# Four attention layers on one core: the second normalising product moves from VectorE to GpSimd

## The chip, the cores and the metric

The kernel runs on one core of a Trainium2 chip. The metric is the device time of one launch in microseconds. The core has a matrix engine (TensorE, PE in the profile, with its weight loads shown as PEld), VectorE (DVE), ScalarE (ACT), GpSimd (POOL) and SyncE (SP). Each engine works through a queue of its own in order, and the engines wait for one another on semaphores. SP, ACT and POOL also issue DMAs; the kernel calls their DMA queues SP, AQ and GQ. A GpSimd instruction and a DMA issued from GpSimd stand in the same physical queue.

## The reference

The input is 2048 tokens of width 1024, bf16, with 32 heads of width 32. Four residual blocks follow one another, A, B, A, B, and the two A blocks share weights, as do the two B blocks.

```
x = x + A(layernorm(x));  x = x + B(layernorm(x))      # twice
A: q, k, v = x @ wqkv;  phi(t) = [softmax(t @ w_phi), softmax(-t @ w_phi)]
   o = (phi(q) @ (phi(k)^T v)) / (phi(q) . sum(phi(k)) + 1e-6);  o @ wo
B: q, k, v = x @ wqkv
   p = softmax(q k^T / sqrt(32));  o = p @ v;  o @ wo
```

Block A is a linear attention and is cheap. Block B is a full softmax attention over 2048 x 2048 scores in each of 32 heads.

## The kernel before

The program is written by a planner. Every piece of work is an `op(engine, planned duration, function, dependencies, buffers, priority)`. The class `Sched` plays the whole program through once on the host, engine by engine, with planned durations, latencies (`LAT`) and buffers that come free (`QUOTA` limits how many of a class live at once), and emits the instructions in the order in which they start in that play. That order is what each hardware queue then holds. The planner treats POOL (instructions) and GQ (DMAs issued by GpSimd) as two engines; the hardware has one queue for both. `TIE` seeds a random draw that multiplies each planned DVE and PE duration by a factor between 0.99 and 1.01; another seed, or another list of DVE and PE operations, gives another order throughout the program.

Activations are held transposed (features on partitions) in chunks of 512 tokens. A block B, in `attention`, is 32 turns: one turn is a query chunk `qc` (4 of them) with a group `g` of four heads (8 of them). A turn has two halves `pp`, and each half 32 units; a unit is the scores of one head, 128 keys by 512 queries.

- Scores: TensorE writes groups of two or three units to PSUM (L1257).
- Exponentials: most groups go to ScalarE (L1273, 1536 or 1024 columns wide). Some units go to VectorE, which computes the exponential with a polynomial (`exp_dve`): `take` reads PSUM (L1184), then five instructions on SBUF follow for a pair of units (L1193, L1196, L1198, L1201, L1203). How many is fixed by the table `COUNT`.
- Weighted sums: TensorE multiplies the exponentials by v and by ones (L1305) into one PSUM bank. After each half VectorE copies that bank to a buffer `T` in SBUF (L1321): 64 partitions hold sums over v and the other 64 the denominators, the other way round in the other half.
- Normalising: four small DMAs gather the denominators of both halves, VectorE takes reciprocals (L1361), one DMA writes them to DRAM and one reads them back spread over the partitions (`bk`). Two products follow (L1370): the first, `k = 1`, over all 128 partitions with the `T` of the second half, and then `k = 0` over the lower 64 partitions with the `T` of the first half. Both write the same bf16 tile `oT`, so the second waits for the first. The lower half of what the first wrote is overwritten.

The last turn of each attention is normalised in another way and has no L1370, so there are 31 turns with two products in each of the two attentions.

The output projection reads `oT` much later in most turns. While the attention runs, TensorE also makes keys, queries and values of later head groups (L530, copied out of PSUM by VectorE at L1057 and L1065). In the first attention there are also layer norms (L691, L695) and the keys of the next block A for three chunks (L820 to L841), where GpSimd casts a column of reciprocals (L841). GpSimd's other work in these stretches is issuing weight loads (L705, L709).

Of the kernel before, what the change touches and what calls it, by code (L numbers as in the profile page):

```python
# [52 lines left out]
OVER = {"DVE": 0.085, "ACT": 0.012}  # L53
NEXT = {"DVE": 0.05, "ACT": 0.13}
RING = 0.5
TIE = 17
LOOK = 8


# [10 lines left out]
class Sched:  # L70
# [11 lines left out]
    def op(self, eng, dur, fn, deps=(), bufs=(), prio=0.0, lat=None, mode=None):  # L82
        o = Op(eng, dur, LAT[eng] if lat is None else lat, fn, tuple(bufs), prio, mode, len(self.ops))
        for d in deps:
            if d is not None:
                d.out.append(o)
                o.ndep += 1
        for b in o.bufs:
            b.left += 1
        if eng == "DVE" and any(b.kind == "ps" and b.banks in ([(7,)], [(6,)]) for b in o.bufs):  # L90
            o.ahead = EVAC
        self.ops.append(o)
        return o
# [76 lines left out]
    def run(self):  # L170
        draw = random.Random(TIE)
        for o in self.ops:
            if TIE and o.eng in ("DVE", "PE"):
                o.dur *= 1 + draw.uniform(-0.01, 0.01)
# [193 lines left out]
def dve_us(n):  # L368
    return n / 960 + 0.15
# [6 lines left out]
def kernel(  # L376
# [11 lines left out]
    nc = tc.nc  # L388
# [95 lines left out]
    op = sch.op  # L484

    def sb(cls, *dims, dt=BF16):
        n = 1
        for d in dims:
            n *= d
        b = Buf("sb", -(-n * (4 if dt == F32 else 2) // 64) * 64, cls)  # L490
        b.with_ = ()

        def v():
            ap = arena[:, b.at // 2:b.at // 2 + n * (2 if dt == F32 else 1)]
            if dt == F32:
                ap = ap.bitcast(F32)
            if len(dims) == 2:
                ap = ap.rearrange("p (a b) -> p a b", a=dims[0])
            elif len(dims) == 3:
                ap = ap.rearrange("p (a b c) -> p a b c", a=dims[0], b=dims[1])  # L500
            return ap

        return b, v
# [707 lines left out]
    def attention(base, kT, vT, q_of, gate, extra):  # L1211
# [69 lines left out]
        if True:  # L1281
            for qc, g in turns:
                T = []
# [43 lines left out]
                r_b, r_v = d_b, d_v  # L1327
                if end:

                    o_b, o_v = sb("oT", C512)  # L1330
# [3 lines left out]
                    s = [op("DVE", dve_us(512), lambda o_v=o_v, r_v=r_v, T=T: nc.vector.tensor_tensor(  # L1334
                        out=o_v()[lo_, :], in0=T[0][1]()[lo_, :], in1=r_v()[hi_, :], op=ALU.mult),
                        rc, [o_b, d_b, T[0][0]], prio)]
# [10 lines left out]
                    s = cut[0] + cut[1][-1:]  # L1347
# [19 lines left out]
                o_b, o_v = sb("oT", C512)  # L1367
                s = []
                for k, a in ((1, slice(0, P)), (0, lo_)):
                    s.append(op("DVE", dve_us(512), lambda a=a, k=k, o_v=o_v, r_v=r_v, T=T: nc.vector.tensor_tensor(  # L1370
                        out=o_v()[a, :], in0=T[k][1]()[a, :], in1=r_v()[a, :], op=ALU.mult),
                        [bk, *s], [o_b, r_b, T[k][0]], prio))
                oTs[qc][g] = (o_b, o_v, s)
# [23 lines left out]
    for layer in range(2):  # L1397
# [48 lines left out]
        for c in range(NC):  # L1446
            pr = second + 20 * c
            o_b, o_v = sb("oc", G, C512)
# [38 lines left out]
        if wide == NC:  # L1487
            for i in range(pos[(2, HALF)], len(turns)):
                qc, g = turns[i]
                pl = at + 10 * i - LATE  # L1490
                wl = slab("w2", pl - 3, B_w[:, :, g * P:(g + 1) * P], P, [q_of[turns[i - 2]][2][0]])
                q_of[(qc, g)] = b_q(g, qc, pl, wl, FIL)
        oTs, last_s = attention(at, kT, vT, q_of, gate, lambda i: PAIRS[COUNT[layer][i]])
        if last:
            bo_s = [slab("slab", at + BO + fc, B_o[:, :, fc * C512:(fc + 1) * C512], C512, [q_of[(1, G - 1)][2][0]])
# [27 lines left out]
        if not last:  # L1523
            r_b, r_v = sb("w2r", 2, D)
# [68 lines left out]
```

## Time and profile before

| | |
|---|---|
| time before, median of 3 runs | 2245.67 us (2244.37 to 2248.56) |
| time of the profiled execution | 2247.36 us |
| its span, first to last instruction | 2245.1 us |
| busy: PE, DVE, ACT, POOL | 2176.1, 1855.9, 1985.7, 197.0 us |
| mean granted TensorE clock | 0.998 |
| first attention's exponentials on ScalarE | from 327 us to the stretch 1200 to 1250 us |
| second attention's exponentials on ScalarE | from the stretch 1400 to 1450 us to 2234 us |

The busy time of an engine is the time in which at least one of its instructions is under way, as a sum over stages with different limits. Durations of neighbouring VectorE instructions overlap a little in the records, so the step from start to start is shorter than the duration. The profiled execution took 2.3 us more than its span, and 1.7 us more than the median.

### The profile page before, as it was taken

The page shows a single profiled execution, that of the slowest core. Times are in us where ns is not written, and L with a number is a line of the kernel's source. Part 1 is how long each engine was busy: PE and PEld are TensorE (multiplying, and loading weights), DVE is VectorE, ACT ScalarE, POOL GpSimd, SP SyncE. Part 2 cuts the span into 40 slices and gives each one's busy share as a digit, 9 for nine tenths or more (in the row PEclk, how much of TensorE's full clock was granted, in tenths as well). Part 3 has the DMA queues.
Part 4 walks back from the last instruction along what each step waited for, and adds up shares of the span by engine and source line. Part 5 has one row for each costly group of instructions (what it writes and reads, how often), then busy time and mean ns, then how long its engine had stood idle before and what let it go on. Part 6 is the DMA issues. An engine that isn't in the chain of part 4 may idle for free.

```text
span 2245.1 us, 82636 instructions
## 1 busy us (share of the span) xinstructions
PE 2176.1 (97%) x36788; PEld 872.2 (39%) x36788; DVE 1855.9 (83%) x2761; ACT 1985.7 (88%) x1939; POOL 197.0 (9%) x299
## 2 busy tenths in 40 slices
PE   7999999999999999999999999999999999999999
PEld 4554454444333333333333444433333333333333
DVE  7986873698899889677887788799999999988968
ACT  4436669999999999999998555999999999999998
POOL 1110000000001010121124200000000000100000
PEclk9999999999999999999999999999999999999999
DMA  9220101111122221222235100111111100211111
GB/s 207 49 81 3 33 24 42 41 34 34 51 57 88 74 73 54 64 96 73 78 110 152 59 5 10 36 37 38 36 29 29 35 24 19 73 31 35 47 36 38
DMA packets 121789, 119.67 MB, mean 53 GB/s; under 512 B 57752, under 2 KB 99800, under 8 KB 121432
## 3 DMA queue, kind: packets, MB, share of 16 engines
q1 hardware_dynamic: 102392, 56.64, 10.0%
q0 software_dynamic: 17424, 56.18, 8.7%
q8 instruction: 287, 4.70, 0.9%
q10 hardware_dynamic: 1616, 1.57, 0.2%
q14 instruction: 70, 0.57, 0.1%
HBM read 79.23 MB, written 14.14 MB: 42 GB/s over the span
## 4 chain that ended last, share of the span: by engine, by line
PE 28%; ACT 23%; DVE 9%; issue 5%; DMA 1%; SPq 0%; ACTq 0%; DVEq 0%
ACT arena L1273 22%; PE psum L530 14%; PE psum L1305 6%; PE psum L1257 6%; DVE arena L1203 2%; DVE arena L1184 1%; DVE arena L1196 1%; DVE arena L1201 1%; DVE arena L1193 1%; ACT arena L823 1%; DMA arena<-arena 1%; DVE arena L1370 1%; DVE arena L1198 1%; DVE arena L1057 1%; PE psum L994 0%
## 5 line engine op out<-in xcount | busy, mean ns | idle before, releaser
L1273 ACT ACTIVATE arena<-psum 128x1536 bf16<-128x1536 f32 (+1 forms) x1366 | 1668.5, 1446 | 12.0 <-PE psum L1257 7.1
L530 PE MATMUL psum<-arena 128*32 128x512 bf16 (+1 forms) x18432 | 1058.3, 358 | 12.5 <-DVE arena L836 2.7
L530 PEld LDWEIGHTS <-arena 128*32 128x32 bf16 x18944 | 459.8, 96 | 447.2 <-issue 175.7
L1305 PE MATMUL psum<-arena 128*32 128x512 bf16 x4096 | 628.1, 383 | 4.0 <-issue 2.0
L1305 PE MATMUL psum<-arena,ones_bf 128*32 128x512 bf16 x4096 | 628.1, 383 | 0.0
L1257 PE MATMUL psum<-arena 32*128 32x512 bf16 x4096 | 536.2, 383 | 27.2 <-ACT arena L1273 22.4
L1257 PEld LDWEIGHTS <-arena 32*128 32x128 bf16 x4096 | 158.4, 91 | 555.8 <-issue 549.0
L1184 DVE TENSOR_SCALAR arena<-psum 128x512 int32<-128x512 f32 x418 | 284.5, 686 | 101.7 <-PE psum L1257 90.3
L1203 DVE SCALAR_TENSOR_TENSOR arena<-arena 128x1024 int16<-128x1024 int32 x209 | 254.7, 1218 | 5.7 <-DVE arena L1201 0.4
L1305 PEld LDWEIGHTS <-arena 128*32 128x32 bf16 x4096 | 163.2, 95 | 227.8 <-issue 177.0
L1305 PEld LDWEIGHTS <-ones_bf 128*32 128x32 bf16 x4096 | 161.3, 95 | 22.3 <-issue 7.9
L705 POOL DMA_DIRECT2D arena<-in_B_wqkv_dram x46 | 42.2, 919 | 1248.6 <-PE psum L530 302.5
L1193 DVE TENSOR_SCALAR arena<-arena 128x1024 f16<-128x1024 int16 x209 | 143.8, 690 | 4.4 <-DMA arena<-arena 0.3
L1196 DVE TENSOR_TENSOR arena<-arena 128x1024 f16<-128x1024 f16 x209 | 142.6, 684 | 4.6
L1201 DVE TENSOR_TENSOR arena<-arena 128x1024 f16<-128x1024 f16 x209 | 142.6, 684 | 3.1
L1057 DVE CAST arena<-psum 128x512 bf16<-128x512 f32 x128 | 87.7, 685 | 57.6 <-PE psum L530 57.3
L823 ACT ACTIVATE arena<-psum 128x512 bf16<-128x512 f32 x80 | 43.0, 596 | 82.6 <-PE psum L530 66.7
L827 DVE TENSOR_REDUCE arena<-arena 128x32 f32<-128x1024 bf16 x64 | 77.0, 1214 | 33.3 <-ACT arena L823 33.2
L530 PE MATMUL psum<-xT,onesD 128*32 128x512 bf16 x1144 | 103.1, 381 | 1.3 <-DVE arena L836 0.7
L1321 DVE COPY arena<-psum 128x512 f32<-128x512 f32 x126 | 86.3, 685 | 15.4 <-PE psum L1305 15.0
L1198 DVE TENSOR_SCALAR arena<-arena 128x1024 f16<-128x1024 f16 x209 | 87.9, 422 | 1.7
L836 DVE TENSOR_TENSOR arena<-psum,arena 128x1024 bf16<-128x1024 f32 x64 | 77.4, 1219 | 13.3 <-PE psum L530 9.7
(124 smaller groups left out, 1383.6 us busy)
## 6 DMA issues: line engine op xcount, KB each, us to landing
arena<-rd SPq DMA_DIRECT2D x62, 256.0 KB
arena<-in_B_wqkv_dram POOLq DMA_DIRECT2D x58, 256.0 KB, 4.1
arena<-in_B_wo_dram POOLq DMA_DIRECT2D x40, 256.0 KB, 4.4
arena<-arena SPq DMA_DIRECT2D x256, 32.0 KB
arena<-wd_k POOLq DMA_DIRECT2D x32, 256.0 KB, 5.0
arena<-in_A_wqkv_dram POOLq DMA_DIRECT2D x32, 256.0 KB, 4.6
arena<-arena SPq DMA_DIRECT2D x96, 64.0 KB
arena<-arena SPq DMA_DIRECT2D x248, 2.0 KB
```

The source lines that it names most:

```text
L530: nc.tensor.matmul(out_[ks, :], lhsT=lhsT[:, ks], rhs=rhs, start=start, stop=stop, tile_position=(0, 32 * k), skip_group_check=True)
L1057: return op("DVE", dve_us(512), lambda: nc.vector.tensor_copy(out=dst(), in_=src()), [dep], bufs, prio)
L1184: o = op("DVE", dve_us(512), lambda: nc.vector.tensor_scalar(out=x_v()[:, k, :].bitcast(I32), in0=s_v()[:, x * C512:(x + 1) * C512], scala ...
L1193: last = op("DVE", 1024 / 1920 + 0.15, lambda: nc.vector.tensor_scalar(out=z(), in0=x_v().bitcast(I16).rearrange("p a (n two) -> p a n two ...
L1196: last = op("DVE", 1024 / 1920 + 0.15, lambda: nc.vector.tensor_tensor(out=u(), in0=z(), in1=z(), op=ALU.mult), [last], [z_b, u_b], prio + ...
L1198: last = op("DVE", 1024 / 3840 + 0.15, lambda: nc.vector.tensor_scalar(out=u(), in0=u(), scalar1=POW2_C[0], scalar2=POW2_C[1], op0=ALU.mul ...
L1201: last = op("DVE", 1024 / 1920 + 0.15, lambda: nc.vector.tensor_tensor(out=u(), in0=z(), in1=u(), op=ALU.mult), [last], [z_b, u_b], prio + ...
L1203: return op("DVE", dve_us(1024), lambda: nc.vector.scalar_tensor_tensor(out=y_v().bitcast(I16), in0=x_v().bitcast(I32), scalar=128.0 / BIT ...
L1257: nc.tensor.matmul(out=s_v()[:, x * C512:(x + 1) * C512], lhsT=kT[g][1]()[r, pp, d * P:(d + 1) * P], rhs=q_of[(qc, g)][1]()[r, (pp + j // ...
L1273: ex = op("ACT", act_us(w * C512), lambda s_v=s_v, e_v=e_v, w=w: nc.scalar.activation(out=e_v(), in_=s_v()[:, 0:w * C512], func=ACT.Exp, s ...
L1305: nc.tensor.matmul(out=a_v()[col:col + 32, :], lhsT=v_v()[:, kc % 4, o:o + DH] if what == 0 else ones_bf[:], rhs=ev()[:, x * C512:(x + 1) ...
L1321: cp = op("DVE", dve_us(512), lambda t_v=t_v, a_v=a_v: nc.vector.tensor_copy(out=t_v(), in_=a_v()), [last], [a_b, t_b], prio - 4)
```

## The change

The second product (`k = 0`, 64 partitions by 512 columns, fp32 times fp32 to bf16, all in SBUF) is given to POOL with a planned duration of 1.3 us, in place of DVE with its planned 0.683 us. The seed `TIE` goes from 17 to 23.

```diff
-TIE = 17
+TIE = 23
...
                 for k, a in ((1, slice(0, P)), (0, lo_)):
-                    s.append(op("DVE", dve_us(512), lambda a=a, k=k, o_v=o_v, r_v=r_v, T=T: nc.vector.tensor_tensor(
+                    s.append(op("DVE" if k else "POOL", dve_us(512) if k else 1.3, lambda a=a, k=k, o_v=o_v, r_v=r_v, T=T: (
+                        nc.vector if k else nc.gpsimd).tensor_tensor(
                         out=o_v()[a, :], in0=T[k][1]()[a, :], in1=r_v()[a, :], op=ALU.mult),
                         [bk, *s], [o_b, r_b, T[k][0]], prio))
```

62 instructions move. Each now waits on a semaphore from VectorE for the first product, and the readers of `oT` wait for GpSimd.

## The prediction

> **What bounds the kernel now.** I read the page first, then the busy times by stretch, then ScalarE's waits, then the chain.
>
> ```profile
> span 2245.1 us, 82636 instructions
> PE 2176.1 (97%) x36788; PEld 872.2 (39%) x36788; DVE 1855.9 (83%) x2761; ACT 1985.7 (88%) x1939; POOL 197.0 (9%) x299
> ```
> ```profile
> core 0: us, PE busy (x) PEld busy (x) DVE busy (x) ACT busy (x) POOL busy (x), PEclk, DMA share, GB/s
> 1450.00:1550.00 100.00, 98.76 (x1505) 35.27 (x1502) 97.07 (x154) 99.57 (x85) 2.67 (x3) 1.00 0.14 33
> 1800.00:1900.00 100.00, 98.40 (x1543) 36.79 (x1543) 92.21 (x145) 100.00 (x86) 0.00 (x0) 1.00 0.09 23
> 900.00:950.00 50.00, 45.33 (x735) 16.00 (x731) 30.99 (x43) 47.03 (x42) 7.93 (x13) 0.97 0.25 71
> 1150.00:1200.00 50.00, 48.73 (x791) 17.73 (x788) 44.42 (x68) 47.11 (x43) 16.29 (x23) 0.97 0.30 85
> ```
> The page gives the base of all shares, 2245.1 us, and shows TensorE, ScalarE and VectorE all high, which an average over stages can't rank. The stretches can (columns: stretch, its length, then busy us and instructions of PE, PEld, DVE, ACT, POOL, then the granted clock). In the second attention ScalarE is busy for 99.57 and 100.00 of 100 us, TensorE for 98.76 and 98.40, VectorE for 97.07 and 92.21. In two stretches of the first attention ScalarE reaches only 47.03 and 47.11 of 50 us, and there the granted clock is 0.97.
>
> ```profile
> L1273 ACT ACTIVATE arena<-psum 128x1536 bf16<-128x1536 f32 (+1 forms) x1366 | 1668.5, 1446 | 12.0 <-PE psum L1257 7.1
> PE psum L1257 <- ACT arena L1273: 22.4, 77, 0.9
> ```
> ScalarE's exponentials stood idle for only 12.0 us in 1366 instructions, and TensorE's scores waited 77 times for ScalarE to free their bank. So ScalarE sets the pace of both attentions. Their exponentials are split between ScalarE and VectorE by a table which the change leaves alone. Work taken from VectorE shortens the run only where VectorE was, for a moment, what the others waited for. The chain tells how often that is:
>
> ```profile
> by line: ACT arena L1273 22.1%; PE psum L530 14.0%; PE psum L1305 6.4%; PE psum L1257 5.8%; issue 5.4%; DVE arena L1203 1.5%; DVE arena L1184 1.1%; DVE arena L1196 1.1%; DVE arena L1201 0.9%; DVE arena L1193 0.9%; ACT arena L823 0.8%; DMA a
> ```
> VectorE's polynomial lines lie on it with 1.5, 1.1, 1.1, 0.9 and 0.9 per cent each: small, but not nothing.
>
> **What leaves VectorE.** These groups show the moved product (64x512, x62) and what stands around it in VectorE's queue. The last figures are busy us, mean ns, idle us before.
>
> ```profile
> L1184 DVE TENSOR_SCALAR arena<-psum 128x512 int32<-128x512 f32 x418 | 284.5, 686 | 101.7 <-PE psum L1257 90.3 <-ACT arena L1273 4.9 <-ACT arena L1056 2.6
> L1203 DVE SCALAR_TENSOR_TENSOR arena<-arena 128x1024 int16<-128x1024 int32 x209 | 254.7, 1218 | 5.7 <-DVE arena L1201 0.4
> L1193 DVE TENSOR_SCALAR arena<-arena 128x1024 f16<-128x1024 int16 x209 | 143.8, 690 | 4.4 <-DMA arena<-arena 0.3
> L1201 DVE TENSOR_TENSOR arena<-arena 128x1024 f16<-128x1024 f16 x209 | 142.6, 684 | 3.1
> L1196 DVE TENSOR_TENSOR arena<-arena 128x1024 f16<-128x1024 f16 x209 | 142.6, 684 | 4.6
> L1198 DVE TENSOR_SCALAR arena<-arena 128x1024 f16<-128x1024 f16 x209 | 87.9, 422 | 1.7
> L1057 DVE CAST arena<-psum 128x512 bf16<-128x512 f32 x128 | 87.7, 685 | 57.6 <-PE psum L530 57.3
> L1321 DVE COPY arena<-psum 128x512 f32<-128x512 f32 x126 | 86.3, 685 | 15.4 <-PE psum L1305 15.0 <-ACT arena L1273 0.2
> L1370 DVE TENSOR_TENSOR arena<-arena 128x512 bf16<-128x512 f32 x62 | 42.1, 679 | 0.9 <-DMA arena<-rd 0.6 <-issue 0.2
> L1370 DVE TENSOR_TENSOR arena<-arena 64x512 bf16<-64x512 f32 x62 | 41.9, 675 | 0.1
> L1065 DVE TENSOR_SCALAR arena<-psum 128x512 bf16<-128x512 f32 x48 | 32.9, 685 | 19.4 <-PE psum L530 16.0 <-DMA arena<-rd 3.2
> ```
> ```profile
> 1621.44 0.68 DVE L1370 TENSOR_TENSOR arena<-arena 128x512 bf16<-128x512 f32 x1
> 1622.04 0.69 DVE L1193 TENSOR_SCALAR arena<-arena 128x1024 f16<-128x1024 int16 x1
> 1622.64 0.68 DVE L1370 TENSOR_TENSOR arena<-arena 64x512 bf16<-64x512 f32 x1
> 1623.25 0.68 DVE L1196 TENSOR_TENSOR arena<-arena 128x1024 f16<-128x1024 f16 x1
> ```
> The moved product lasts 675 ns, but from 1622.64 to 1623.25 it takes 0.61 us of the queue, and neighbours of its kind 0.60. So 62 x 0.60 = 37.2 us of VectorE's time go. The idle time before it is 0.1 us in all, so no wait goes with it. What it is worth is its share of the chain:
>
> ```profile
> 720.91 0.60 DVE arena L1370
> ...
> 2176.16 0.60 DVE arena L1370
> ```
> These are the first and the last of 15 pieces of the chain (start, us) that are second products; they sum to 8.2 us, 22% of 37.2. If nothing else changed, the gain would be at most 8.2 us, and less where ScalarE or TensorE is right behind.
>
> **What GpSimd needs for it.** The trace of before has no product of two SBUF tensors on GpSimd. The nearest rows:
>
> ```profile
> masks.py:199 POOL TENSOR_SCALAR_AFFINE_SELECT ident<-ident 128x128 bf16<-128x128 bf16 x1 | 0.3, 287 | 0.1
> L1577 POOL MEMSET const-bfloat16-1.0<- 128x1 bf16 x1 | 0.1, 101 | 0.0
> ```
> A row of 128 columns with one input takes 287 ns, and an instruction of one column 101 ns. That is (287 - 101) / 127 = 1.46 ns a column; 512 columns make 101 + 511 x 1.46 = 0.85 us for one input, and twice the column price, for two inputs, 1.60 us. I take 1.2 us, about the middle. The Trainium skill, GPSIMD Engine Reference, section Performance versus the Vector engine, gives about 2.6 cycles an element for two inputs, by which I estimate 512 x 2.6 / 1.2 GHz = 1.1 us plus dispatch; no run here shows it yet.
>
> GpSimd has time: it is busy 197.0 us of the run. The readers of `oT` are not in a hurry even at the end, where the margin is least:
>
> ```profile
> 2230.33 0.69 DVE L1370 TENSOR_TENSOR arena<-arena 128x512 bf16<-128x512 f32 x1
> 2232.19 0.67 DVE L1370 TENSOR_TENSOR arena<-arena 64x512 bf16<-64x512 f32 x1
> 2236.95 0.77 DVE L1344 TENSOR_TENSOR arena<-psum,arena 64x256 bf16<-64x256 f32 x2 [2.39 <-ACT arena L1342]
> ```
> At the end of the run the first product ends at 2231.02 and the second starts only at 2232.19, because another copy lies between. GpSimd could start right behind the first and end near 2231.1 + 1.2 = 2232.3 (2232.7 by the long price), ahead of today's 2232.86. Nor does the last turn's own product (L1344, at 2236.95) come any later, as it waits for ScalarE. I cost the tail at nothing; that cover holds as long as GpSimd's product ends before about 2236, and a product later than that moves the end by its lateness.
>
> **What it does to VectorE's other work.** This is the term that decides. The trace has both directions of a conflict between the two engines.
>
> ```profile
> L841 POOL CAST arena<-arena x64: 321/330/1129, 34.8 to 1261.0; 128x32 bf16<-128x32 f32 x64
> 100.09 1.16 DVE L695 TENSOR_TENSOR arena<-arena 128x1024 bf16<-128x1024 f32 x1
> 100.31 1.13 POOL L841 CAST arena<-arena 128x32 bf16<-128x32 f32 x1 [4.93 <-DVE arena L830]
> ```
> ```profile
> 1747.32 1.40 POOL L705 DMA_DIRECT2D arena<-in_B_wqkv_dram  x1 [50.78 <-DVE arena L1184]
> 1748.14 1.07 DVE L1193 TENSOR_SCALAR arena<-arena 128x1024 f16<-128x1024 int16 x1
> ```
> GpSimd's small cast (L841; min, median, max ns) takes 330 ns as a rule. The one at 100.31 took 1.13 us and ended at 101.44, 0.19 us after VectorE's L695 (two SBUF inputs) had ended at 101.25. GpSimd waited for the whole instruction. In the other direction VectorE's L1193, which takes 690 ns on average, took 1.07 us while GpSimd issued a DMA: 0.38 us were lost.
>
> So the two can't read together where VectorE has two SBUF inputs, or streams SBUF to SBUF at the pace of L1193 and L1198. In the groups above these are L1203, L1193, L1196, L1201, L1198 (5 x 209) and L1370 (124), 1169 instructions. Those that read PSUM are L1184, L1057, L1321 and L1065 (418 + 128 + 126 + 48 = 720). So 62% use what GpSimd needs. The product starts while VectorE goes on with its queue. If the next instruction that VectorE starts is of the first kind (0.62) it waits about 1.2 us. If not, it runs for 0.60 us, and the one behind it waits the other 0.60 us with a chance of 0.62: 0.38 x 0.62 x 0.60 = 0.14. Together 0.744 + 0.141 = 0.885 us a turn, 54.9 us in all, more than the 37.2 us saved. That takes the lock to hold both ways alike. The low end is the stretch that the trace shows, 0.38 us: 62 x 0.62 x 0.38 = 14.6 us.
>
> The Trainium skill, SBUF — State Buffer, section Who interferes with whom, speaks against this change: a VectorE instruction with two SBUF inputs contends with a GpSimd instruction that reads SBUF, and whichever issues second blocks fully. The cast's 1.13 us agree with it for GpSimd as the second; for VectorE as the second no row here shows more than 0.38 us. By the rule the block is the 54.9 us, and without it the 14.6 us.
>
> What does blocked time cost? By the chain, L1203, L1193, L1196 and L1201 hold 1.5 + 0.9 + 1.1 + 0.9 = 4.4% of 2245.1 = 98.8 us there, of 254.7 + 143.8 + 142.6 + 142.6 = 683.7 us busy: 14%. The second product itself had 22%. The blocked instructions stand in the same places of the queue, and the planner's order now counts on a VectorE that is free 0.68 us earlier, so what is late is late against the order, with TensorE's in-order queue behind it. I take 22%: 54.9 x 0.22 = 12.1 us lost. The ends are 14.6 x 0.14 = 2.0 us and twice my share, 24.2 us.
>
> **What is queued behind GpSimd's wait.** The product waits in GpSimd's queue for `bk` and for the first product. Behind it stand weight loads (L705, L709) and, in the first attention, 24 casts (L841), which the kv sums and the buffers of ScalarE's L823 need. Today that reads:
>
> ```profile
> ACT arena L823 <- POOL arena L841: 4.7, 2, 2.4
> ```
> Two waits, 4.7 us. One in four of the 24 casts behind a product of 1.2 us would add 7 us of delay on GpSimd, of which at 14 to 22% some 1 to 1.5 us arrive. I take 1 us.
>
> **Sum.** - 8.2 + 12.1 + 1 = + 4.9 us. On the profiled execution's own 2247.36 us that is 2252.3; it lay 1.7 us above the median of the runs, so against 2245.67 I forecast 2250.6 us. What a measurement of this kernel can tell from no change is about 0.2%, 4.5 us; the forecast is just beyond it.
>
> **Rivals.** First, the relief lands. The block is only the 0.38 us seen in L1193, and the DVE time saved counts: - 8.2 + 14.6 x 0.22 + 1 = - 4.0 us, 2241.7; with no block at all - 8.2, 2237.5. For it speaks that no row shows VectorE losing more than 0.38 us; against it, that GpSimd waited out a whole instruction, and one lock should work both ways. It decides where the block is under 0.60 us a turn.
>
> Second, ScalarE hides all. The exponentials were idle for 12.0 us of 1668.5, and VectorE's lateness of under a microsecond ends in ScalarE's two sets of banks: 2245.7, plus or minus 2 us. For it speaks the 99.57 to 100.00 of 100; against it, the 8.2 us of second products on the chain.
>
> Third, the change doesn't do what it says: moving 62 operations and the seed redraw the order of the whole program, and what is measured is the redraw. The two stretches where ScalarE reached 47.03 and 47.11 of 50 us hold 2.97 + 2.89 = 5.9 us; an order without such holes would give 2239.8, and one with as many more 2251.6. Nothing in the profile says which.
>
> Fourth, GpSimd's queue. Where `bk` lands late, the product holds a weight load back, and TensorE's in-order queue stands still for it, at the price of such a stretch, 2.9 us, and more where the clock falls. Five of those make + 14.7, 2260.4. Against it: the first product was idle for only 0.6 us for that DMA in the whole run.
>
> **Chances.** The block as forecast, slower: 0.33; the queue: 0.05; the relief: 0.18; hidden: 0.20. The redraw alone takes 0.24: 0.12 faster, 0.08 slower, 0.04 within. That makes faster 0.30, same 0.24, slower 0.46. The range: low end the full relief with a little of a good redraw, 2236; high end the block at the doubled share (- 8.2 + 24.2 + 1 = + 17.0, 2262.7), 2263. The forecast's own case alone would span 2247 to 2263.
>
> **What would show it.** In the profile of the changed kernel: a GpSimd product x62 at L1371 or so with a mean of 1.0 to 1.6 us (longer where it waited); VectorE's groups L1193, L1196, L1198, L1201, L1203 with means up by some 30 to 50 ns each (54.9 us over 1045 instructions is 53 ns), while L1184 and L1321 keep their 686 and 685 ns. If these means stand still, the block is wrong and the relief right. If they rise and the time does not, ScalarE hides it. If the time differs while stretches outside the attentions (before 327 us, and from 1215 to 1420 us) make the difference, it is the redraw. GpSimd's waits for L1370 with weight loads behind them and TensorE idle there would show the queue. The prediction is wrong if the time comes out under 2241 us, or if the products sit on the chain themselves.

## The result, and the profile after

The changed kernel takes 2280.89 us (median of 4 runs, 2279.76 to 2283.03) against 2245.97 us before: a ratio of 1.0160, with a 95% interval of 1.0145 to 1.0175. It is 35 us slower by the medians, 36 by the ratio. The direction was forecast; the size was not, and the time lies 18 us above the range.

The page of the changed kernel, span, engines, ScalarE's exponentials and the moved product:

```profile
span 2280.1 us, 82872 instructions
PE 2180.6 (96%) x36800; PEld 867.0 (38%) x36800; DVE 1859.2 (82%) x2699; ACT 1995.0 (87%) x1939; POOL 289.2 (13%) x361
L1273 ACT ACTIVATE arena<-psum 128x1536 bf16<-128x1536 f32 (+1 forms) x1366 | 1674.7, 1382 | 32.2 <-PE psum L1257 14.4
L1371 POOL TENSOR_TENSOR arena<-arena 64x512 bf16<-64x512 f32 x62 | 90.3, 1456 | 937.0 <-DVE arena L1371 745.9
```

The exponentials on ScalarE, the same 1366, now stand idle for 32.2 us where it was 12.0. The product on GpSimd (L1371 in this kernel) lasts 1456 ns on average. The same two stretches of the second attention as before, in the same columns:

```profile
1450.00:1550.00 100.00, 96.47 (x1490) 34.83 (x1487) 94.92 (x144) 96.81 (x82) 6.85 (x5) 1.00 0.12 30
1800.00:1900.00 100.00, 97.25 (x1563) 36.93 (x1566) 91.95 (x142) 97.81 (x82) 4.38 (x3) 1.00 0.09 24
```

ScalarE fell from 99.57 and 100.00 to 96.81 and 97.81 of 100 us. VectorE, which gave work away, is hardly less busy than it was: 94.92 against 97.07 us in the first stretch and 91.95 against 92.21 in the second. Its groups say what fills the time:

```profile
L1203 DVE SCALAR_TENSOR_TENSOR arena<-arena 128x1024 int16<-128x1024 int32 x209 | 257.1, 1230 | 6.7 <-DMA arena<-arena 1.1 <-DVE arena L1201 0.8 <-ACT arena L1273 0.8
L1193 DVE TENSOR_SCALAR arena<-arena 128x1024 f16<-128x1024 int16 x209 | 163.1, 782 | 5.6 <-DMA arena<-arena 1.0 <-POOL arena L1371 0.6
L1196 DVE TENSOR_TENSOR arena<-arena 128x1024 f16<-128x1024 f16 x209 | 148.0, 709 | 6.6 <-DMA arena<-arena 0.6
L1201 DVE TENSOR_TENSOR arena<-arena 128x1024 f16<-128x1024 f16 x209 | 147.8, 708 | 2.9
L1198 DVE TENSOR_SCALAR arena<-arena 128x1024 f16<-128x1024 f16 x209 | 93.6, 449 | 2.1
L1184 DVE TENSOR_SCALAR arena<-psum 128x512 int32<-128x512 f32 x418 | 284.3, 685 | 112.0 <-PE psum L1257 99.0 <-ACT arena L1273 9.6 <-ACT arena L823 1.3
L1321 DVE COPY arena<-psum 128x512 f32<-128x512 f32 x126 | 86.1, 683 | 16.0 <-PE psum L1305 15.9
```

The five instructions on SBUF are longer: by 12, 92, 25, 24 and 27 ns on average, against 1218, 690, 684, 684 and 422 before. Times 209 that is 37.6 us. The two that read PSUM (L1184, L1321) stand at 685 and 683 ns, as before. One turn shows how it comes about, VectorE's rows first and then GpSimd's:

```profile
786.24 0.68 DVE L1371 TENSOR_TENSOR arena<-arena 128x512 bf16<-128x512 f32 x1
786.84 0.68 DVE L1201 TENSOR_TENSOR arena<-arena 128x1024 f16<-128x1024 f16 x1
787.44 1.76 DVE L1193 TENSOR_SCALAR arena<-arena 128x1024 f16<-128x1024 int16 x1
787.06 1.58 POOL L1371 TENSOR_TENSOR arena<-arena 64x512 bf16<-64x512 f32 x1 [24.11 <-DVE arena L1371]
```

The first product ends on VectorE at 786.92. GpSimd's instruction begins at 787.06, while L1201 (two SBUF inputs) is under way until 787.52. It ends at 788.64: 1.58 us, 0.32 more than the shortest of the 62 took. L1193, issued by VectorE at 787.44, lasts 1.76 us in place of 0.69 and ends 0.56 us after GpSimd's product. I read this as GpSimd waiting for VectorE's instruction, and then VectorE waiting for GpSimd's. The product by itself, and L1196 (two SBUF inputs), in min, median and max ns:

```profile
L1371 POOL TENSOR_TENSOR arena<-arena x62: 1259/1280/2732, 381.3 to 2265.9; 64x512 bf16<-64x512 f32 x62
L1196 DVE TENSOR_TENSOR arena<-arena x209: 621/685/1766, 387.2 to 2256.9; 128x1024 f16<-128x1024 f16 x105
```

Counted over the whole trace by start and end, 50 of the five groups' instructions started while a product was under way, and they took 34 us longer than their medians, 0.7 us each.

What came late then is seen in TensorE's waits. Before, it waited for VectorE's copies so long (us, times, longest):

```profile
PE psum L1305 <- DVE arena L1321: 1.1, 5, 0.3
PE psum L530 <- DVE arena L1057: 1.6, 7, 0.4
```

and in the changed kernel:

```profile
PE psum L1305 <- DVE arena L1321: 8.0, 20, 0.8
PE psum L530 <- DVE arena L1057: 7.4, 17, 1.0
PE psum L530 <- DVE arena L1065: 4.7, 11, 0.8
```

By stage, taken from the first and the last exponential on ScalarE in the traces: the first attention went from 885.6 to 900.2 us, the second from 822.4 to 839.5 us, and the stretch between them from 199.8 to 200.9 us. The loss lies in the two attentions.

### The profile page after: what moved, and what is told of

It reads as the page before. It is cut to its first block, busy times and chain, and to the rows that moved or that the text cites. A ratio compares the mean times of both kernels' runs of the same rounds, so it can differ in the third digit from the quotient of the medians.

```text
span 2280.1 us, 82872 instructions
## 1 busy us (share of the span) xinstructions
PE 2180.6 (96%) x36800; PEld 867.0 (38%) x36800; DVE 1859.2 (82%) x2699; ACT 1995.0 (87%) x1939; POOL 289.2 (13%) x361
## 5 line engine op out<-in xcount | busy, mean ns | idle before, releaser
L1273 ACT ACTIVATE arena<-psum 128x1536 bf16<-128x1536 f32 (+1 forms) x1366 | 1674.7, 1382 | 32.2 <-PE psum L1257 14.4
L530 PE MATMUL psum<-arena 128*32 128x512 bf16 (+1 forms) x18432 | 1057.7, 357 | 31.7 <-DVE arena L1057 7.4
L1184 DVE TENSOR_SCALAR arena<-psum 128x512 int32<-128x512 f32 x418 | 284.3, 685 | 112.0 <-PE psum L1257 99.0
L1371 POOL TENSOR_TENSOR arena<-arena 64x512 bf16<-64x512 f32 x62 | 90.3, 1456 | 937.0 <-DVE arena L1371 745.9
L1193 DVE TENSOR_SCALAR arena<-arena 128x1024 f16<-128x1024 int16 x209 | 163.1, 782 | 5.6 <-DMA arena<-arena 1.0
L1196 DVE TENSOR_TENSOR arena<-arena 128x1024 f16<-128x1024 f16 x209 | 148.0, 709 | 6.6 <-DMA arena<-arena 0.6
L1201 DVE TENSOR_TENSOR arena<-arena 128x1024 f16<-128x1024 f16 x209 | 147.8, 708 | 2.9
L1321 DVE COPY arena<-psum 128x512 f32<-128x512 f32 x126 | 86.1, 683 | 16.0 <-PE psum L1305 15.9
L1198 DVE TENSOR_SCALAR arena<-arena 128x1024 f16<-128x1024 f16 x209 | 93.6, 449 | 2.1
```

The lines of the kernel that those rows point to most:

```text
L530: nc.tensor.matmul(out_[ks, :], lhsT=lhsT[:, ks], rhs=rhs, start=start, stop=stop, tile_position=(0, 32 * k), skip_group_check=True)
L1184: o = op("DVE", dve_us(512), lambda: nc.vector.tensor_scalar(out=x_v()[:, k, :].bitcast(I32), in0=s_v()[:, x * C512:(x + 1) * C512], scala ...
L1193: last = op("DVE", 1024 / 1920 + 0.15, lambda: nc.vector.tensor_scalar(out=z(), in0=x_v().bitcast(I16).rearrange("p a (n two) -> p a n two ...
L1196: last = op("DVE", 1024 / 1920 + 0.15, lambda: nc.vector.tensor_tensor(out=u(), in0=z(), in1=z(), op=ALU.mult), [last], [z_b, u_b], prio + ...
L1198: last = op("DVE", 1024 / 3840 + 0.15, lambda: nc.vector.tensor_scalar(out=u(), in0=u(), scalar1=POW2_C[0], scalar2=POW2_C[1], op0=ALU.mul ...
L1201: last = op("DVE", 1024 / 1920 + 0.15, lambda: nc.vector.tensor_tensor(out=u(), in0=z(), in1=u(), op=ALU.mult), [last], [z_b, u_b], prio + ...
```

## Experiments

Three accounts stood against one another: the lock (GpSimd's reading holds up VectorE), the order (the planner wrote an order that counts on the relief), and the redraw (another order is better or worse by chance). Ratios below are to the kernel before on the same chip, with 95% intervals; 0.1% is 2.2 us. The edits are shown shortened to the instructions that they change.

### Seed alone

```diff
-TIE = 17
+TIE = 23
```

> The kernel before with the seed 23 in place of 17, both products on VectorE. Lock theory (GpSimd's product holds what VectorE's instructions need, and their delay is what costs): within 6 us of before, 2240 to 2252. Redraw theory (the order written with seed 23 costs, whatever engine does the product): 2270 to 2285. Order theory (the planner's order counts on relief that VectorE does not get): 2240 to 2252, since here VectorE has its planned work.

2289.08 us, 1.0196 (1.0180 to 1.0211). The old kernel with the new seed is slower than the changed kernel. The redraw account alone allowed for a slower kernel, and the time lies above even its 2270 to 2285; the price is many times the 5.9 us that the prediction gave it. Two more seeds tell whether 23 is odd.

> The kernel before with seed 1. If orders scatter and the one of seed 17 lies at the low end: 2260 to 2295. If 23 is an unlucky seed and 17 an ordinary one: 2240 to 2255.

> The kernel before with seed 2. As for seed 1: 2260 to 2295 if seed 17 lies at the low end of a wide scatter, 2240 to 2255 if seed 23 is the odd one.

Seed 1: 2275.66 us, 1.0130 (1.0107 to 1.0153). Seed 2: 2257.6 us, 1.0053 (1.0038 to 1.0068). Seed 1 falls into the range for a wide scatter, seed 2 between the two ranges. Of four orders of the same work that of the kernel before is the fastest, and they spread over nearly 2%. In the profiled executions the loss lies mainly between the attentions: from the last exponential to the next first one it is 199.8 us with seed 17, 206.7 with seed 2, 226.5 with seed 1 and 228.5 with seed 23 (there with another 13 us in the attentions). The kv sums (L856) between 1200 and 1450 us say why, for seeds 17, 2, 1 and 23 (busy us and number of TensorE's matmuls, then the same for its weight loads):

```profile
1200.00:1450.00 250.00, 2.62 (x256) 2.55 (x256) 0.99 0.15 43
```
```profile
1200.00:1450.00 250.00, 3.10 (x305) 2.79 (x293) 0.99 0.19 55
```
```profile
1200.00:1450.00 250.00, 3.85 (x384) 3.79 (x384) 0.99 0.19 55
```
```profile
1200.00:1450.00 250.00, 5.09 (x512) 4.58 (x512) 0.99 0.23 70
```

There are 256 (one chunk), 305, 384 and 512 of these matmuls in that stretch: with seeds 1 and 23 half a chunk and a whole chunk more of block A's keys have not found room under the first attention, and are done where no exponentials run beside them.

### GpSimd with the old seed, and with the old factors

> The changed kernel with the old seed 17. Lock theory: 2272 to 2290, VectorE's L1193, L1196, L1198, L1201 and L1203 again some 35 to 40 us longer in sum than before. Redraw theory: near 2246 if the seed is what costs. Order theory: 2265 to 2290 as well, since this order counts on the relief too.

2286.47 us, 1.0182 (1.0167 to 1.0197). The stretch on VectorE is there again, 37 us, and the lock and the order account both allowed for this time. The seed 23 by itself is not what costs: with 17 the redraw account expected some 2246.

```diff
-            if TIE and o.eng in ("DVE", "PE"):
-                o.dur *= 1 + draw.uniform(-0.01, 0.01)
+            if TIE and o.eng in ("DVE", "PE") or o.eng == "POOL" and o.dur == 1.3:
+                f = 1 + draw.uniform(-0.01, 0.01)
+                if o.eng != "POOL":
+                    o.dur *= f
```

> The changed kernel with seed 17, where the 62 moved operations still take their number from the draw without using it, so that every other operation has the factor that it has in the kernel before. The planner's order differs from before only by what the move itself changes in its play. Redraw theory (the random factors make the order good or bad): the order is mostly that of before, 2250 to 2260, the 8.7 us of the GpSimd product included. If any departure from the order of before costs, whatever the factors: 2270 to 2290.

2295.48 us, 1.0213 (1.0192 to 1.0234), above even the second range. Keeping every factor does not keep the order: the move alone sets the planner's play on another course. What is redrawn isn't the factors, it is the order.

### The same order, the other engine

```diff
-                        nc.vector if k else nc.gpsimd).tensor_tensor(
+                        nc.vector if k else nc.vector).tensor_tensor(
```

> The changed kernel's order, with the second product at the same place of that order but done by VectorE. TensorE's list of instructions is the same as in the changed kernel. Lock theory: the stretch of L1193 and its neighbours is gone, and the time falls to 2245 to 2258, a little above before because VectorE has 37 us more than this order plans. Order theory and redraw theory: 2272 to 2295, as slow as the changed kernel or slower.

2272.28 us, 1.0120 (1.0102 to 1.0138): 14 us above the lock account's range, at the low end of the other. The conflict is gone,

```profile
L1273 ACT ACTIVATE arena<-psum 128x1536 bf16<-128x1536 f32 (+1 forms) x1366 | 1673.8, 1378 | 25.8 <-PE psum L1257 13.3 <-DVE arena L1203 2.8 <-PE psum L530 1.5
L1193 DVE TENSOR_SCALAR arena<-arena 128x1024 f16<-128x1024 int16 x209 | 144.0, 690 | 4.9 <-DMA arena<-arena 1.0
```

with L1193 back at 690 ns, yet the exponentials still stand idle for 25.8 us. In this order VectorE has 37 us of work that the order did not plan for it. In this order GpSimd is 0.4% worse than VectorE (1.0160 against 1.0120), some 9 us.

The mirror image is the order of before with the product on GpSimd; the lists of TensorE are equal.

```diff
-  lambda a=a, k=k, ...: nc.vector.tensor_tensor(
+  lambda a=a, k=k, ...: (nc.vector if k else nc.gpsimd).tensor_tensor(
```

> The order of before, with the second product alone done by GpSimd in place of VectorE. TensorE's list is the same as before. Lock theory: VectorE's SBUF instructions stretch by 30 to 45 us in sum, it is spared 37 us, and the time is 2260 to 2285. Order theory and redraw theory: the order is that of before and VectorE is relieved against it, 2238 to 2250.

2254.23 us, 1.0039 (1.0024 to 1.0054), below what the lock account gave and above what the others gave.

```profile
L1273 ACT ACTIVATE arena<-psum 128x1536 bf16<-128x1536 f32 (+1 forms) x1366 | 1671.4, 1413 | 13.5 <-PE psum L1257 7.2 <-PE psum L1305 1.2 <-PE psum L856 1.1
L1203 DVE SCALAR_TENSOR_TENSOR arena<-arena 128x1024 int16<-128x1024 int32 x209 | 258.9, 1239 | 6.1 <-DVE arena L1201 0.4 <-PE psum L1305 0.2
L1193 DVE TENSOR_SCALAR arena<-arena 128x1024 f16<-128x1024 int16 x209 | 147.9, 710 | 5.7 <-PE psum L1257 0.6 <-DMA arena<-arena 0.5 <-POOL arena L1370 0.2
L1196 DVE TENSOR_TENSOR arena<-arena 128x1024 f16<-128x1024 f16 x209 | 147.9, 709 | 6.1 <-POOL arena L1370 0.5 <-PE psum L1257 0.5
L1201 DVE TENSOR_TENSOR arena<-arena 128x1024 f16<-128x1024 f16 x209 | 147.4, 707 | 3.2
L1198 DVE TENSOR_SCALAR arena<-arena 128x1024 f16<-128x1024 f16 x209 | 101.0, 485 | 2.0
```

VectorE's five groups are longer by 21, 20, 25, 23 and 63 ns, 31.8 us in sum, but the exponentials' idle time hardly moves, 13.5 against 12.0 us. The other engine costs 8.8 us in this order, as in the other. The rest of the 35 us comes with the changed order: what that order costs, and what the product costs more in it than in this one.

### Taking away the conflict, not the move

GpSimd writes a constant into the same tile. The order stays, and so do GpSimd's wait for the first product and TensorE's waits for GpSimd; the reads go. With them go the waits of instructions that later reuse the memory which GpSimd read: in the traces 55 VectorE instructions wait for GpSimd's semaphore in place of 99, and 32 of ScalarE's in place of 77. Those waits cost little in the changed kernel (us, times, longest):

```profile
DVE arena L1193 <- POOL arena L1371: 0.6, 1, 0.6
POOL arena L705 <- POOL arena L1371: 0.5, 2, 0.3
ACT arena L1273 <- POOL arena L1371: 0.3, 1, 0.3
```

```diff
-    nc.gpsimd.tensor_tensor(out=o_v()[a, :], in0=T[k][1]()[a, :], in1=r_v()[a, :], op=ALU.mult)
+    nc.gpsimd.memset(o_v()[a, :], 0.0078125)
```

> The changed kernel and its order, with GpSimd's product replaced by a constant written to the same 64x512 tile: GpSimd reads nothing of SBUF, every wait and the order stay, and the lower half of oT is not the attention's. Lock theory: the conflict goes with the reads; the stretch of L1193, L1196, L1198, L1201 and L1203 (37.7 us in the changed kernel) falls under 8 us and the time by 8 to 15 us, to 2266 to 2273, no further, since the order's cost stays. Had the lock been all of it, the time would fall to 2240 to 2248. If the reads were not what counts: 2278 to 2284.

2255.99 us, 1.0044 (1.0026 to 1.0063): lower than the lock account had it, and not down to before.

```profile
L1273 ACT ACTIVATE arena<-psum 128x1536 bf16<-128x1536 f32 (+1 forms) x1366 | 1670.0, 1405 | 15.0 <-PE psum L1257 7.6 <-PE psum L1305 1.4 <-DMA rd<-arena 1.1
L1193 DVE TENSOR_SCALAR arena<-arena 128x1024 f16<-128x1024 int16 x209 | 146.9, 704 | 5.0 <-DMA arena<-arena 1.0
L1196 DVE TENSOR_TENSOR arena<-arena 128x1024 f16<-128x1024 f16 x209 | 142.7, 684 | 7.1 <-DMA arena<-arena 0.5 <-ACT arena L1273 0.5 <-PE psum L1257 0.5
L1372 POOL MEMSET arena<- 64x512 bf16 x62 | 35.3, 569 | 947.0 <-DVE arena L1370 871.0 <-ACT arena L1273 68.1 <-PE psum L1257 4.5
```

L1196 is back at 684 ns, L1193 nearly so, the five groups are 3.4 us longer than before in place of 37.6, and the exponentials stand idle for 15.0 us. Against the changed kernel's 1.0160 the conflict costs 1.16%, 26 us, in this order. The write is shorter than the product, so a control makes it as long:

```diff
+    for _ in range(3):
         nc.gpsimd.memset(o_v()[a, :], 0.0078125)
```

> The changed kernel with three constant writes in a row on GpSimd in place of its product, some 1.5 us each turn against 0.57 us with one write: GpSimd is busy as long as with the product but reads nothing; the lower half of oT is not the attention's. If the reads of SBUF are what costs: 2254 to 2262, as with one write. If GpSimd's time, its queue or the late oT is what costs: 2272 to 2284.

2260.93 us, 1.0062 (1.0040 to 1.0084), as expected if the reads cost. (Here and in the runs with half a product and with two, a helper function holds the products: GpSimd's stands at L1216, the first at L1213, and lines behind it have numbers 7 or 8 higher.)

```profile
L1193 DVE TENSOR_SCALAR arena<-arena 128x1024 f16<-128x1024 int16 x209 | 153.1, 734 | 4.7 <-DMA arena<-arena 0.6
L1216 POOL MEMSET arena<- 64x512 bf16 x186 | 115.0, 618 | 919.5 <-DVE arena L1213 772.9 <-ACT arena L1280 111.8 <-DVE arena L1198 23.4
```

Three writes of 618 ns each keep GpSimd busy for 115 us in all, more than the product's 90.3, and the time is that of one write within the intervals. So it is neither GpSimd's time, nor its queue, nor a late `oT`: the reads cost, 26 us against one write and 22 against three.

```diff
+    h = slice(0, 256)
-    nc.gpsimd.tensor_tensor(out=o_v()[a, :], in0=T[k][1]()[a, :], in1=r_v()[a, :], op=ALU.mult)
+    nc.gpsimd.tensor_tensor(out=o_v()[a, h], in0=T[k][1]()[a, h], in1=r_v()[a, h], op=ALU.mult)
+    nc.gpsimd.memset(o_v()[a, 256:512], 0.0078125)
```

> The changed kernel with GpSimd's product over 256 of the 512 columns and a constant written to the others (that part of oT is not the attention's). If the cost goes with the length of the reading: half of the 25 us between one constant write and the whole product, 2265 to 2272. If one conflict costs the same whatever its length: 2277 to 2283.

2264.8 us, 1.0079 (1.0055 to 1.0102), just under the expected 2265 to 2272.

```profile
L1193 DVE TENSOR_SCALAR arena<-arena 128x1024 f16<-128x1024 int16 x209 | 157.6, 756 | 4.1
L1216 POOL TENSOR_TENSOR arena<-arena 64x256 bf16<-64x256 f32 x62 | 57.8, 932 | 932.4 <-DVE arena L1213 774.7 <-ACT arena L1281 98.6 <-PE psum L1265 27.4
```

L1193 lies between (756 against 704 and 782 ns), and the cost is 0.35% over one write, 8 us, where the whole product costs 26. The five groups' stretch halves: 16.9 us over one write, against 34 with the whole product. The cost grows with the length of the reading, and perhaps faster than it; half of it, 1.0102, is the end of the interval.

The same two questions in the order of before. First the relief without the conflict (the edit of the constant write, in the kernel before):

> The order of before with the second product replaced by a constant written by GpSimd (the lower half of oT is not the attention's): VectorE is relieved and nothing locks. The prediction's first term: 8.2 us faster at most, 2238 to 2244. If the relief is worth what it was in the changed kernel's order, 16 us: 2229 to 2235. If ScalarE hides it: 2244 to 2248.

2247.79 us, 1.0005 (0.9994 to 1.0016). VectorE is rid of 62 products, nothing holds it up, and nothing is gained:

```profile
L1273 ACT ACTIVATE arena<-psum 128x1536 bf16<-128x1536 f32 (+1 forms) x1366 | 1668.1, 1449 | 13.0 <-PE psum L1257 8.6 <-PE psum L1305 2.5 <-issue 0.3
```

The exponentials stand idle for 13.0 us, as they did (12.0). The prediction's first term, 8.2 us at most, is nil here; ScalarE hides it. So in this order the conflict is worth 1.0039 less 1.0005, 8 us. In the profiled executions only 3.5 us of it lie in the attentions; 2.7 lie ahead of the first exponential, where no product runs.

```diff
+    for _ in range(2):
         nc.gpsimd.tensor_tensor(out=o_v()[a, :], in0=T[k][1]()[a, :], in1=r_v()[a, :], op=ALU.mult)
```

> The order of before with the second product done twice over by GpSimd. Lock theory: the second reading brings as much conflict as the first: if the order of before gains 4 to 8 us from the relief, one lock costs 13 to 17 us there, and two give 2266 to 2274; the stretch of VectorE's SBUF instructions doubles from 31.5 us to some 60. If the loss of 8.8 us with one product was not the lock's: 2252 to 2257.

2306.05 us, 1.0266 (1.0233 to 1.0299), far over what any account gave.

```profile
L1193 DVE TENSOR_SCALAR arena<-arena 128x1024 f16<-128x1024 int16 x209 | 164.9, 790 | 24.6 <-POOL arena L1216 19.6 <-PE psum L1264 0.2 <-DMA arena<-arena 0.2
L1196 DVE TENSOR_TENSOR arena<-arena 128x1024 f16<-128x1024 f16 x209 | 151.4, 726 | 9.5 <-POOL arena L1216 3.9 <-PE psum L1312 0.4 <-issue 0.3
```

The stretch about doubles as expected (57 us for the five groups; L1193 by 100 ns, L1196 by 42), but there is a second thing that was not expected: VectorE stands idle before L1193 and L1196 for 19.6 and 3.9 us until GpSimd is done, and ScalarE's exponentials for 12.5 us. I take this to be reuse of memory: the order lets buffers that the product reads go at VectorE's pace, and what is written next into that space waits for GpSimd. The trace names who is waited for, not why, so this stays argued. As a measure of the lock's price the run is spoiled by it.

### A second order that plans the relief

The conflict cost 26 us in one order and 8 us in another. The order of the changed kernel with seed 17 (1.0182 with GpSimd's product) is a second one in which the relief is planned.

> The changed kernel with seed 17 (1.0182 of before) with GpSimd's product replaced by a constant write: no reads, same order; the lower half of oT is not the attention's. If the conflict costs 20 to 26 us in any order that plans the relief: 2258 to 2268. If the changed kernel's own order was odd and the conflict is worth the 9 us of the order of before: 2274 to 2282.

> The order of the changed kernel with seed 17, the second product done by VectorE at its place in that order. If, as with seed 23, VectorE's unplanned 37 us cost 11 to 16 us beyond the write alone and GpSimd's conflict 9 us more than that: 2271 to 2283. If GpSimd is no worse than VectorE once the order is another: 2284 to 2290.

With the constant write 2260.71 us, 1.0054 (1.0039 to 1.0069); with the product on VectorE 2274.35 us, 1.0115 (1.0093 to 1.0137). Both lie in the first of their two ranges, and the pattern holds:

| ratio to before | constant write | product on VectorE | product on GpSimd |
|---|---|---|---|
| order of before | 1.0005 | 1 | 1.0039 |
| order of the changed kernel | 1.0044 | 1.0120 | 1.0160 |
| the same with seed 17 | 1.0054 | 1.0115 | 1.0182 |

Along each row only the engine and the reads differ. In the orders that plan the relief the conflict costs 1.16 and 1.28% (26 and 29 us), the same product on VectorE 0.76 and 0.61% (17 and 14 us), so GpSimd is the worse place by 9 to 15 us. The first column is what the order alone costs: 10 and 12 us over before, with all of the relief in it.

The stages of the profiled executions show where (us against before, from the first and last exponentials as above):

| order, second product | ahead of the first exponential | the two attentions | between them |
|---|---|---|---|
| of before, constant write | + 0.3 | + 0.7 | - 0.5 |
| of before, GpSimd | + 3.0 | + 4.2 | + 0.1 |
| changed, constant write | + 2.7 | + 8.0 | + 1.7 |
| changed, VectorE | + 0.5 | + 23.2 | + 1.1 |
| changed, GpSimd | + 1.2 | + 31.7 | + 1.1 |
| seed 17, constant write | + 0.7 | + 1.1 | + 10.4 |
| seed 17, VectorE | + 0.6 | + 17.1 | + 9.1 |
| seed 17, GpSimd | + 2.1 | + 25.8 | + 12.2 |

The first column is scatter of single executions, up to 3 us. In the attentions the conflict costs 24 and 25 us in the two orders that plan the relief, and 3.5 in the order of before. What the order alone costs is not one thing: in the changed kernel's order (seed 23) most of it lies in the attentions, with seed 17 nearly all of it between them, where the prediction's own sign of a redraw points.

## Why the prediction was wrong, by its own steps

- **What bounds the kernel.** Right: ScalarE sets the pace of both attentions, and the whole loss but some 3 us lies in them.
- **The relief, 8.2 us at most.** Mis-sized. In the order of before it is worth nothing (1.0005, 0.9994 to 1.0016). The share of a line in the chain that ended last was read as time that would go with the line; but ScalarE is so close behind that it took over each time. In the orders that plan it, the product on VectorE costs 14 to 17 us over the constant write.
- **GpSimd's duration, 1.2 us.** Right: 1.26 us where it isn't held up, 1.46 on average. The Trainium skill's rule of about 2.6 cycles an element (GPSIMD Engine Reference, Performance versus the Vector engine), by which the estimate was 1.1 us plus dispatch, agrees with it.
- **The block on VectorE, 54.9 us.** The mechanism is right and was the one named as deciding: the five SBUF groups are longer and the PSUM groups are not. The sum was too large: 37.6 us in place of 54.9. About as many instructions were held as its chances make (50, against 53), but for 0.7 us on average, not up to 1.2. The Trainium skill's rule (SBUF — State Buffer, Who interferes with whom) that of a VectorE instruction with two SBUF inputs and a GpSimd instruction that reads SBUF the second to issue blocks fully agrees with L1196, which took up to 1766 ns, 1.08 us over its median, behind a product. Writing alone, which by the same section does not contend with two SBUF inputs, left L1196 at 684 ns. L1193 at 787.44 has one input, so it is no case of that rule, and it was held as long.
- **What blocked time costs, 22%.** This is the step that failed: it took the price from the chain of the order of before. In that order it was near: 8 us of the 31.8, 25% (3.5 us by the attentions alone, 11%). In the order that the change really brings it is 26 us of the 37.6, 69% (23.7 us, 63%). That the two orders that plan the relief leave VectorE less slack is shown by the middle column of the ratios: its own product, which costs nothing in the order of before, costs 14 to 17 us there. Why they do is open. They spend the relief that they plan; but they are also simply other orders, and no run puts the write and the product into another order of the unchanged kernel. Why a block costs still more than an equal amount of VectorE's own work is argued only: it comes in pieces of up to 1.1 us. For that speaks that three writes, which stretch the five groups by 9.7 us more than one does in pieces of up to 0.4 us, cost 1 us more in the attentions, and the half product, with 16.9 us, 9 us.
- **The redraw, 5.9 us either way.** This failed as well, by far, as it went into the sum at nothing. Two visible holes in the profile were taken for the scatter of orders. Other seeds of the unchanged kernel gave + 12, + 29 and + 44 us (0.53, 1.30 and 1.96%), by another distribution of whole pieces of work over the stages. The order of before was at the fast end, which no row of a single profile can tell. In the changed kernel's order with the constant write the order accounts for 10 us.
- **The tail at nothing, the queue at 1 us.** The tail holds within a microsecond: 11.0 us from the last exponential to the end, against 10.2. GpSimd's queue showed no cost: three writes in it cost no more than one.

Of the 36 us (1.60%), 10 are the order with the relief in it and 26 the conflict (by the longer control 14 and 22). The prediction had + 4.9. In the order of before GpSimd's product costs 8.8 us, so there + 4.9 would have been near, but by luck: a relief that does not come, 8.2, against a block priced 4 us too high and a queue that shows no cost. None of the versions run beats the kernel before.

## What to carry to other kernels

Where a planner writes the program, moving one operation is also a new order: price the two apart, by running the new engine in the old order and the old engine in the new one, before saying what the move is worth. Before offloading from VectorE to GpSimd, ask whether what GpSimd reads holds up what VectorE reads meanwhile; a constant write in the product's place shows that part by itself. And work taken from an engine that wasn't the bound gave nothing here in the order it had, while the same time lost on it cost most of itself in another order.

## What was not expected of the hardware

In the changed kernel L1193, with a single input (SBUF to SBUF), suffered most from GpSimd's product: longer by 92 ns on average, against 25 and 24 for L1196 and L1201 with two inputs. That is mostly a matter of which instruction stands behind the product: 21 of the 50 that started while a product was under way were L1193. In the order of before it was L1198, also with a single input, that suffered most (63 ns, against 20 for L1193). One hold was alike for both kinds: up to 1.08 us longer than the median for L1193, L1196 and L1198, where they started behind a product.

With writes the kinds differ. GpSimd's constant writes stretched the single-input L1193 to 704 ns with one write and 734 with three, and L1198 from 422 to 427 and 439, while L1196 stood at 684 and 686 and L1201 at 682 and 683.
